# Queries and keys split in place instead of through DRAM, and a second chunk of feed-forward work tied to attention items

## The chip, the cores and the metric

One core of a Trainium2 chip runs the whole program. The metric is device time in microseconds of one execution; the kernel before took 875.44 us (median of 3 runs, 873.63 to 877.91). Engines are named as in the profile: PE (matmuls) with PEld (its weight loads), DVE, ACT, POOL, and SP, which here only issues DMAs. Each engine takes its instructions strictly in the order in which the program lists them, so one that waits holds up all behind it on that engine.

## The reference

Four batches of 576 tokens, 8 heads of 64. Causal attention with a bias from a running sum of gates, then a two-matmul feed-forward mix with a gate, then a mixer over tokens and channels:

```python
scores = scale * np.matmul(q, k.transpose(0, 1, 3, 2))
scores = np.where(causal, -1e9, scores + np.minimum(bias, 0.0))
attn = softmax(scores)
x = np.matmul(attn, v)                       # to [batch, 576, 512]
k = np.maximum((mu_k * x + (1 - mu_k) * x_prev) @ w_k, 0.0)
v = k * k @ w_v
r = sigmoid((mu_r * x + (1 - mu_r) * x_prev) @ w_r)
x = r * v                                    # then the token and channel mixer
```

## The kernel before

**Numbers in two parts.** To get float32 results from PE's faster format (F32R), a number is split in a high part (a copy rounded to F32R) and a low part (the number less its high part). A product is then three matmuls: high by high, high by low, low by high (`products`, L103 to L109). Queries and keys of batches 1 to 3 are split in the same way, but there the three products share two matmuls, since a head has only 64 rows of the 128 that a matmul sums over. X1 holds the high queries and keys in one half of the partitions and in the other half 4 rows for the bias (from ext_d in DRAM) and zeros. X2 holds high queries and low queries against low keys and high keys. `scores` (L294 to L312) issues one matmul on X1 (L307) and one on X2 (L308) for each block. There are two X1 and two X2, used in turn: even visits have the first, odd visits the second.

**Visits and items.** A visit is one head of batches 1 to 3, 24 in all. An item is one block of 128 query rows of a visit. An even visit has five items, of 128, 256, 384, 512 and 576 columns; the fifth holds the last 64 rows of two heads at once, its own and the next visit's, so the odd visit has four. The fifth item's scores come in two parts of 288 columns, and `maskp` masks the second. Each item runs through a chain: scores on PE, `softmax_max` on DVE (L278), the exponential on ACT (L289), the sum's reciprocal (POOL L290, DVE L291), the normalisation on POOL (L292), transposes on PE (L435, L450), their split on ACT and DVE, and the product with the values on PE (L493). Batch 0's attention (L392, L401, L421) comes before and runs unsplit.

**Where queries and keys come from.** Two heads are treated together, in four quarters: queries or keys, 288 columns at a time, 128 partitions. `load` (L227 to L231) brings a quarter from qk to half of a buffer PB. `split` (L233 to L240) makes the high part on ACT (the helper's L75) and the low part on POOL (L239), and SP stores both to hl_d in DRAM (L240). `place` (L260 to L269) later fills a visit's X1 and X2 by four DMAs: the bias rows (L266) and three from hl_d (L267 to L269). PB shares one place (tag HX) with the early heads' queries and keys and with the first chunk's mixed input, so the first load comes after the last matmul on HX.

**Feed-forward work.** Each batch has two chunks of rows (256 and 320). A chunk is 8 `up`, 4 `gate` and 8 half `down` units, 12 matmuls each; its matmuls are at L108, on XK, XR and KK. `mix` (DVE, ACT) makes the input of a chunk from attention's result, so a batch's units can begin when its attention is done. They are spread over the items of the next batch's attention by `todo`, and are what PE does while an item's softmax runs on the other engines. starts and ends (L792) shift the batches' ranges in items.

**What sets the order.** Instructions are written with a place: `with at(x)` gives all inside a priority, and a scheduler, which simulates the engines, lists for each engine what is ready by that priority. An item n has place N0 + n, its transposes N0 + n + 1.5, a feed-forward unit of item n N0 + n + 3. Something of low priority is taken earlier where an engine would stand idle in that simulation. The lists are then fixed, and on the chip each engine follows its own.

Of the kernel before, what the change touches and what calls it, by code (L numbers as in the profile page):

```python
# [8 lines left out]
F32 = mybir.dt.float32  # L9
# [5 lines left out]
ALU = mybir.AluOpType  # L15
# [4 lines left out]
def f32(ap):  # L20
    return ap.bitcast(F32)
# [3 lines left out]
def attention_moe_mixer(  # L25
# [72 lines left out]
    ext_d = dram.tile([G, 4, 2, S], F32, name="ext_d")  # L98
    hl_d = dram.tile([G - H, D, 4, S], F32, name="hl_d")
    y_d = dram.tile([B, DM, S], F32, name="y_d")  # L100
# [21 lines left out]
    VS = v_p.tile([128, NS, 2 * D], F32, name="VS")  # L122
    maskp = v_p.tile([128, S // 2], BF16, name="maskp")

# [16 lines left out]

    X1, X2, PT, VV = {}, {}, {}, {}

    xt = {}

    def constants():
        nc.gpsimd.affine_select(
            out=maskc[:, 512:640], in_=maskc[:, 512:640], pattern=[[-1, 128]],
            compare_op=ALU.is_ge, fill=-8.0e9, base=0, channel_multiplier=1,
        )  # L150
        make_identity(nc, ident)
        nc.gpsimd.memset(maskp, 0.0)
        nc.gpsimd.tensor_copy(maskp[0:TAIL, S // 2 - TAIL:], maskc[0:TAIL, 512:512 + TAIL])
        nc.scalar.dma_start(out=maskp[TAIL:2 * TAIL, S // 2 - TAIL:], in_=maskc[0:TAIL, 512:512 + TAIL])

# [59 lines left out]

    qk_raw = {}

    def stage():
        if "PB" not in act:
            act["PB"] = qk_p.tile([128, 8 * QC], F32, tag="HX", name="PB")  # L220
        return act["PB"]

    def part(y):
        x, c = divmod(y, 2)
        return x, S * c // 2, S * (c + 1) // 2

    def load(i, y):  # L227
        g = visits[i][0]
        x, c0, c1 = part(y)
        t = qk_raw[i, y] = stage()[:, y % 2 * S // 2:(y % 2 + 1) * S // 2]  # L230
        nc.sync.dma_start(out=t, in_=qk[g:g + 2, :, x, c0:c1].rearrange("h d s -> (h d) s"))  # L231

    def split(i, y):  # L233
        g = visits[i][0] - H
        x, c0, c1 = part(y)
        t = qk_raw.pop((i, y))
        e = stage()[:, S + y % 2 * S:S + y % 2 * S + S].rearrange("p (t s) -> p t s", t=2)
        copy("A", e[:, 1].bitcast(F32R), t)
        nc.gpsimd.tensor_tensor(out=e[:, 0], in0=t, in1=e[:, 1], op=ALU.subtract)  # L239
        nc.sync.dma_start(out=hl_d[g:g + 2, :, 2 * x:2 * x + 2, c0:c1].rearrange("h d t s -> (h d) t s"), in_=e)  # L240

# [18 lines left out]
    def place(i):  # L260
        g = visits[i][0]
        t = hl_d[g - H]
        if i < 2:
            X2[i] = x_tile(2 + i, F32R)
        x1, x2 = xs(i)
        nc.sync.dma_start(out=f32(x1[0:4]), in_=ext_d[g])  # L266
        nc.sync.dma_start(out=f32(x1[64:128]), in_=t[:, 1:4:2])  # L267
        nc.sync.dma_start(out=f32(x2[0:64]), in_=t[:, 0:4:3])
        nc.sync.dma_start(out=f32(x2[64:128]), in_=t[:, 1:3])  # L269

# [23 lines left out]
    def scores(i, j):  # L294
        pair = j == NS - 1
        w = 128 * j + (TAIL if pair else 128)
        m = 128
        q0 = 128 * j
        P = p_p.tile([128, w], F32, tag=f"P{j}", name=f"P{j}")
        mx = st_p.tile([128, 2], F32, tag="mx", name="mx")  # L300
        parts = [(0, w // 2), (w // 2, w)] if pair else [(0, w)]
        for x, (c0, c1) in enumerate(parts):
            ps = ps_s.tile([128, 512], F32, tag="s", name="s")
            for e in (1, 0) if pair else (0,):
                x1, x2 = xs(i + e)
                n, a = (TAIL * (1 + e), S - TAIL * (1 + e)) if pair else (128, q0)
                nc.tensor.matmul(ps[0:n, 0:c1 - c0], x1[:, 0, a:a + n], x1[:, 1, c0:c1], start=True, stop=False)  # L307
                nc.tensor.matmul(ps[0:n, 0:c1 - c0], x2[:, 0, a:a + n], x2[:, 1, c0:c1], start=False, stop=True)  # L308
            softmax_max(j, ps, P, mx, x, c0, c1, None if not pair else maskp if x else maskc[:, 0:c1])
        softmax(j, P, mx, x, pair)  # L310
        pst[i, j] = P

# [69 lines left out]
    def late(h, j):  # L382
# [7 lines left out]
        for y, (c0, c1) in enumerate(parts):  # L390
            ps = ps_s.tile([128, 512], F32, tag="s", name="s")
            nc.tensor.matmul(ps[0:m, 0:c1 - c0], x[0:D + 4, 0, q0:q0 + m], x[0:D + 4, 1, c0:c1], start=True, stop=True)  # L392
            softmax_max(j, ps, P, mx, y, c0, c1)
        softmax(j, P, mx, y)
        if j == QC // 128:
# [249 lines left out]
    def attention_item(n):  # L645
        if n < N1:
# [4 lines left out]
            if j == 2 and h > 1 and h % 2 == 0 and h // 2 + 1 < H // 2:  # L651
                with at(N0 + n):
                    late_values(h // 2 + 1)
            if h >= H - 4:
                x = 3 * (h - H + 4) + j - 2
                with at(N0 + n + 0.1):
                    if x >= 4 and x < 8:
                        split(0, x - 4)
                    if x in (2, 3, 4, 5):
                        load(0, x - 2)  # L660
                    if x == 8:
                        load_v(0)
                    if x in (10, 11):
                        load(2, x - 10)
            if h == H - 1 and j == 3:
                with at(N0 + n + 0.2):
                    split_v(0)
            if h == H - 2 and j == 2:
                with at(N0 + n):
                    for x in range(2):  # L670
                        X1[x] = x_tile(x, F32R)
                        nc.gpsimd.memset(f32(X1[x][0:64]), 0.0)
            if h == H - 1 and j == 2:
# [10 lines left out]
        if j == 0 and i + 1 < len(visits):  # L684
            with at(N0 + n):
                place(i + 1)
        if i % 2 == 0:
            with at(N0 + n + 0.1):
                if j < 4 and i + 2 < len(visits):
                    split(i + 2, j)  # L690
                    if j < 2:
                        load(i + 2, 2 + j)
                if j == NS - 1 and i + 2 < len(visits):
                    load_v(i + 2)
        else:
            with at(N0 + n + 0.1):
                if 2 <= j < 4 and i + 3 < len(visits):
                    load(i + 3, j - 2)
            if j == 1 and i + 1 < len(visits):
                with at(N0 + n + 0.2):  # L700
                    split_v(i + 1)
        with at(N0 + n):
# [88 lines left out]
    base = (NS - 2) * H  # L791
    starts, ends = [0, 2, 4, 4], [2, 4, 4, 4]  # L792
    for b in range(B):
# [230 lines left out]
```

## Time and profile before

| | |
|---|---|
| time of the profiled execution | 872.6 us |
| its span, first to last instruction | 870.8 us |
| median of 3 runs | 875.44 us |
| busy share of the span: PE, PEld | 97%, 91% |
| DVE, ACT, POOL | 56%, 52%, 39% |
| mean granted clock of PE | 0.992 |
| DMA traffic | 108.36 MB, mean 124 GB/s |

The page's slices show PE busy nearly throughout, with DVE, ACT and POOL at some 60 to 80% until about 440 us, where attention ends, and falling off afterwards, while the mixer's matmuls fill PE to the end. In a view of waits, a row says which engine, tile and line waited, for what, how many us in total, how often, and the longest. In a view of time, a row has start, duration, engine, line, and in brackets the idle time just before and what ended it. Matmuls are pipelined, so a busy PE is not a PE at its peak.

### The profile page before, as it was taken

The numbers are of one execution on the slowest core, as the hardware profiler recorded it, in microseconds if no ns is written. First come the engines' busy times: TensorE is split into PE (matmuls) and PEld (weight loads), VectorE is DVE, ScalarE is ACT, GpSimd is POOL, SyncE is SP. The second block draws the span as 40 slices with busy tenths as digits, with TensorE's granted clock in tenths as the row PEclk, the third lists the DMA queues.
The fourth block names the chain that finished last, engine by engine and source line by source line (L and its number), as shares of the span: only waits on it lengthen the run. The fifth ranks groups of instructions, "written<-read, shape, count | busy, mean of one in ns | idle before, by whom it ended". The sixth has DMA issues, their size and how long they took to land. (4 is left out here: it accounts for less than half of the span.)

```text
span 870.8 us, 17455 instructions
## 1 busy us (share of the span) xinstructions
PE 840.6 (97%) x6127; PEld 790.5 (91%) x6127; DVE 485.1 (56%) x1352; ACT 452.6 (52%) x1257; POOL 343.4 (39%) x601
## 2 busy tenths in 40 slices
PE   8889998999899999999999999999999999999998
PEld 5656777988789999999999989999999999999998
DVE  5797776565879566985469757951331222222221
ACT  4688766865886656868377865840310221211210
POOL 4565666864785544645256854720000000000000
PEclk9899999999999999999999999999999999999999
DMA  7943778687974244431234746553021112112100
GB/s 191 266 134 88 199 218 230 192 240 210 252 204 133 70 111 117 100 93 41 83 94 129 230 143 217 177 181 94 7 92 54 44 31 74 42 32 73 38 25 26
DMA packets 88024, 108.36 MB, mean 124 GB/s; under 512 B 11152, under 2 KB 71568, under 8 KB 87936
## 3 DMA queue, kind: packets, MB, share of 16 engines
q1 hardware_dynamic: 81408, 91.56, 37.7%
q0 software_dynamic: 4576, 15.08, 5.5%
q8 instruction: 49, 0.80, 0.4%
q10 hardware_dynamic: 1952, 0.60, 0.3%
q14 instruction: 39, 0.32, 0.1%
HBM read 77.74 MB, written 28.90 MB: 122 GB/s over the span
## 5 line engine op out<-in xcount | busy, mean ns | idle before, releaser
L863 ACT ACTIVATE HID<-c 128x256 fp32r<-128x256 f32 (+1 forms) x96 | 39.3, 410 | 220.9 <-PE c L108 220.8
L108 PE MATMUL vd<-KK,WV 128*128 128x256 f32 (+1 forms) x768 | 120.9, 300 | 0.1
L108 PEld LDWEIGHTS vd<-KK,WV 128*128 128x128 f32 x768 | 106.6, 188 | 2.4 <-issue 0.9
L292 POOL TENSOR_SCALAR P<-P,sum 128x128 f32<-128x128 f32 (+4 forms) x148 | 93.6, 636 | 36.2 <-DVE sum L291 30.2
L108 PE MATMUL h<-XK,WK 128*128 128x320 f32 (+1 forms) x672 | 105.9, 303 | 0.7 <-DVE XK L517 0.5
L108 PE MATMUL c<-HID,WV 128*128 128x256 f32 (+1 forms) x768 | 104.9, 291 | 0.0
L108 PE MATMUL c<-U,WK 128*128 128x256 f32 (+1 forms) x768 | 103.2, 291 | 1.4 <-DVE HID L864 1.4
L289 ACT ACTIVATE P<-P,mx 128x128 f32<-128x128 f32 (+4 forms) x148 | 86.9, 588 | 30.3 <-DVE mx L278 23.0
L108 PEld LDWEIGHTS c<-HID,WV 128*128 128x128 f32 x768 | 100.6, 188 | 0.0
L108 PEld LDWEIGHTS c<-U,WK 128*128 128x128 f32 x768 | 98.6, 188 | 1.7 <-DVE HID L864 1.7
L108 PEld LDWEIGHTS h<-XK,WK 128*128 128x128 f32 x672 | 93.8, 189 | 2.1 <-DVE XK L517 0.7
L864 DVE SCALAR_TENSOR_TENSOR HID<-c,HID 128x256 fp32r<-128x256 f32 (+1 forms) x96 | 43.8, 456 | 81.1 <-ACT HID L863 81.0
L278 DVE CUSTOM_DVE_ANT_0 P<-s,maskc 128x128 f32<-128x128 f32 (+4 forms) x148 | 69.1, 478 | 22.1 <-PE t L435 8.4
L928 DVE TENSOR_TENSOR ut<-c,ut 128x256 f32<-128x256 f32 (+1 forms) x32 | 14.6, 458 | 119.3 <-PE c L108 112.0
L529 POOL TENSOR_TENSOR KK<-k,KK 128x256 fp32r<-128x256 f32 (+1 forms) x64 | 55.8, 877 | 19.8 <-ACT k L528 18.7
L108 PE MATMUL r<-XR,WR 128*128 128x320 f32 (+1 forms) x384 | 60.0, 299 | 0.0
L290 POOL TENSOR_SCALAR sum<-sum 128x1 f32<-128x1 f32 (+1 forms) x148 | 32.4, 219 | 67.6 <-ACT P L289 57.2
L108 PE MATMUL c<-HID,WR 128*128 128x256 f32 (+1 forms) x384 | 54.8, 291 | 0.0
L108 PEld LDWEIGHTS r<-XR,WR 128*128 128x128 f32 x384 | 52.8, 188 | 1.1 <-ACT raw L614 0.4
L108 PE MATMUL c<-U,C1A 128*128 128x256 f32 (+1 forms) x384 | 52.8, 296 | 0.1
L108 PEld LDWEIGHTS c<-U,C1A 128*128 128x128 f32 x384 | 51.5, 190 | 0.3 <-ACT U L913 0.3
L108 PEld LDWEIGHTS c<-HID,WR 128*128 128x128 f32 x384 | 51.3, 188 | 0.0
(133 smaller groups left out, 1658.4 us busy)
## 6 DMA issues: line engine op xcount, KB each, us to landing
X<-hl_d SPq DMA_DIRECT2D x72, 288.0 KB
hl_d<-PB SPq DMA_DIRECT2D x48, 288.0 KB
raw<-in_moe_w_ch_dram POOLq DMA_DIRECT2D x48, 256.0 KB, 3.3
PB<-in_qk_dram SPq DMA_DIRECT2D x48, 144.0 KB
yt<-y_d SPq DMA_DIRECT2D x16, 288.0 KB
u_d<-yt SPq DMA_DIRECT2D x16, 288.0 KB
raw<-in_moe_w_k_dram SPq DMA_DIRECT2D x8, 512.0 KB
raw<-in_moe_w_v_dram SPq DMA_DIRECT2D x16, 256.0 KB
```

The source lines that it names most:

```text
L108: nc.tensor.matmul(ps, a, b, start=first and i == 0, stop=last and i == n - 1)
L278: nc.vector.tensor_tensor_reduce(out=P[0:m, c0:c1], in0=ps[0:m, 0:c1 - c0], in1=mask[0:m], scale=-scale, scalar=3.0e38 if x == 0 else mx[0 ...
L289: nc.scalar.activation(out=P[0:m, 0:w], in_=P[0:m, 0:w], func=AF.Exp, bias=mx[0:m, x:x + 1], scale=-1.0, accum_out=sm[0:m, 0:1])
L290: nc.gpsimd.tensor_scalar(out=sm[0:m, 0:1], in0=sm[0:m, 0:1], scalar1=1e-9, scalar2=1.0, op0=ALU.add, op1=ALU.mult)
L292: nc.gpsimd.tensor_scalar(out=P[0:m, 0:w], in0=P[0:m, 0:w], scalar1=sm[0:m, 1:2], scalar2=1.0, op0=ALU.mult, op1=ALU.mult)
L529: nc.gpsimd.tensor_tensor(out=kk[:, 1, m, 0:n], in0=t[:, 0:n], in1=f32(kk[:, 0, m, 0:n]), op=ALU.subtract)
L863: nc.scalar.activation(out=hi, in_=ps, func=AF.Relu)
L864: nc.vector.scalar_tensor_tensor(out=lo, in0=ps, scalar=0.0, in1=f32(hi), op0=ALU.max, op1=ALU.subtract)
L928: nc.vector.tensor_tensor(out=t, in0=ps, in1=t, op=ALU.add)
```

## The change

`split`, hl_d and the quarters go. `load` brings a head's whole queries and keys in one DMA to one half of the partitions of a buffer RQ. `place` splits from there: ACT copies the high part straight into X1, a DMA copies it on to its place in X2, and POOL writes the low part into X2 in two pieces of 288 columns; keys first, then queries. Then it issues the load for the visit after the next one. Even visits have their queries and keys in the lower half of X1, odd ones in the upper half. The fifth item's two parts become 512 and 64 columns. Batch 0's second chunk is spread over 43 items instead of 37, batch 1's units begin 6 items later, and the PE instructions of batch 0's second chunk may not come ahead of the last score matmul of their item (`issue_after`).

```diff
-    maskp = v_p.tile([128, S // 2], BF16, name="maskp")
+    maskp = v_p.tile([128, TAIL], BF16, name="maskp")
+    heads = []
...
-    def load(i, y):
-        g = visits[i][0]
-        x, c0, c1 = part(y)
-        t = qk_raw[i, y] = stage()[:, y % 2 * S // 2:(y % 2 + 1) * S // 2]
-        nc.sync.dma_start(out=t, in_=qk[g:g + 2, :, x, c0:c1].rearrange("h d s -> (h d) s"))
-
-    def split(i, y):
-        g = visits[i][0] - H
-        x, c0, c1 = part(y)
-        t = qk_raw.pop((i, y))
-        e = stage()[:, S + y % 2 * S:S + y % 2 * S + S].rearrange("p (t s) -> p t s", t=2)
-        copy("A", e[:, 1].bitcast(F32R), t)
-        nc.gpsimd.tensor_tensor(out=e[:, 0], in0=t, in1=e[:, 1], op=ALU.subtract)
-        nc.sync.dma_start(out=hl_d[g:g + 2, :, 2 * x:2 * x + 2, c0:c1].rearrange("h d t s -> (h d) t s"), in_=e)
+    def sides(i):
+        a, z = slice(0, D), slice(D, 2 * D)
+        return (a, z) if i % 2 == 0 else (z, a)
+
+    def raw_qk():
+        if "RQ" not in act:
+            act["RQ"] = qk_p.tile([128, 8 * QC], F32, tag="HX", name="RQ")
+        return act["RQ"][:, 0:2 * S].rearrange("p (t s) -> p t s", t=2)
+
+    def load(i):
+        nc.sync.dma_start(out=raw_qk()[sides(i)[0]], in_=qk[visits[i][0]])
...
     def place(i):
         g = visits[i][0]
-        t = hl_d[g - H]
...
-        nc.sync.dma_start(out=f32(x1[0:4]), in_=ext_d[g])
-        nc.sync.dma_start(out=f32(x1[64:128]), in_=t[:, 1:4:2])
-        nc.sync.dma_start(out=f32(x2[0:64]), in_=t[:, 0:4:3])
-        nc.sync.dma_start(out=f32(x2[64:128]), in_=t[:, 1:3])
+        a, z = sides(i)
+        rq = raw_qk()[a]
+        nc.sync.dma_start(out=f32(x1[z][0:4]), in_=ext_d[g])
+        for y in (1, 0):
+            nc.scalar.activation(out=x1[a, y], in_=rq[:, y], func=AF.Copy)
+            high, low = (z, a) if y else (a, z)
+            nc.sync.dma_start(out=f32(x2[high, y]), in_=f32(x1[a, y]))
+            for c in range(2):
+                cs = slice(S * c // 2, S * (c + 1) // 2)
+                nc.gpsimd.tensor_tensor(out=x2[low, y, cs], in0=rq[:, y, cs], in1=f32(x1[a, y, cs]), op=ALU.subtract)
+        if i + 2 < len(visits):
+            load(i + 2)
...
-        parts = [(0, w // 2), (w // 2, w)] if pair else [(0, w)]
+        parts = [(0, 128 * j), (128 * j, w)] if pair else [(0, w)]
...
-                nc.tensor.matmul(ps[0:n, 0:c1 - c0], x2[:, 0, a:a + n], x2[:, 1, c0:c1], start=False, stop=True)
+                mm = nc.tensor.matmul(ps[0:n, 0:c1 - c0], x2[:, 0, a:a + n], x2[:, 1, c0:c1], start=False, stop=True)
...
+        heads.append(mm.ins)
...
-            if h >= H - 4:
-                x = 3 * (h - H + 4) + j - 2
+            if h == H - 3 and j == 2:
                 with at(N0 + n + 0.1):
...
+                    load(0)
+                    load(1)
+            if h == H - 2 and j == 4:
+                with at(N0 + n + 0.1):
+                    load_v(0)
...
-                        nc.gpsimd.memset(f32(X1[x][0:64]), 0.0)
+                        nc.gpsimd.memset(f32(X1[x][sides(x)[1]]), 0.0)
...
-        if i % 2 == 0:
+        if i % 2 == 0 and j == NS - 1 and i + 2 < len(visits):
             with at(N0 + n + 0.1):
-                if j < 4 and i + 2 < len(visits):
-                    split(i + 2, j)
-                    if j < 2:
-                        load(i + 2, 2 + j)
-                if j == NS - 1 and i + 2 < len(visits):
-                    load_v(i + 2)
...
-    starts, ends = [0, 2, 4, 4], [2, 4, 4, 4]
+    starts, ends = [0, 8, 4, 4], [8, 4, 4, 4]
+    tied = set()
...
+                tied.add(id(acts))
...
-            with at(N0 + n + 3):
+            with at(N0 + n + 3), tc.issue_after(heads[n - 0]) if id(acts) in tied else ExitStack():
                 run(acts)
```

## Rows read from the trace of the kernel before

**Rows 1.** Busy us (and instructions) of each engine by stretch; clock, DMA share, GB/s
```profile
core 0: us, PE busy (x) PEld busy (x) DVE busy (x) ACT busy (x) POOL busy (x), PEclk, DMA share, GB/s
125.00:275.00 150.00, 138.70 (x978) 127.36 (x978) 105.77 (x343) 108.01 (x307) 103.77 (x190) 0.99 0.77 211
...
275.00:425.00 150.00, 149.93 (x1135) 148.19 (x1135) 104.03 (x330) 103.50 (x280) 74.16 (x143) 1.00 0.34 85
...
437.00:600.00 163.00, 158.20 (x1125) 155.73 (x1124) 112.75 (x244) 102.78 (x295) 88.71 (x125) 1.00 0.52 162
```

**Rows 2.** Waits of ACT, POOL and PE from 125 to 275 us
```profile
ACT PB L75 <- DMA PB<-in_qk_dram: 27.5, 20, 3.6
...
POOL PB L239 <- ACT PB L75: 16.5, 12, 3.2
...
PE s L308 <- DMA X<-hl_d: 4.1, 3, 2.3
```

**Rows 3.** Waits of SP's queue from 87 to 275 us
```profile
SPq L240 <- POOL PB L239: 31.4, 16, 4.7
```

**Rows 4.** In order of time, 224 to 246 us: one late load
```profile
225.40 0.34 SPq L231 DMA_DIRECT2D PB<-in_qk_dram  x1
...
227.62 0.44 ACT L75 ACTIVATE PB<-PB 128x288 fp32r<-128x288 f32 x1 [0.99 <-DMA PB<-in_qk_dram]
...
228.20 0.79 POOL L239 TENSOR_TENSOR PB<-PB 128x288 f32<-128x288 f32 x1 [1.29 <-ACT PB L75]
...
229.40 0.33 PE L435 MATMUL t<-ident,P 128*128 128x128 f32 x1 [1.34 <-POOL P L292]
```

**Rows 5.** In order of time, 143.5 to 147.5 us: one direct wait for X
```profile
145.57 0.60 SPq L269 DMA_DIRECT2D X<-hl_d  x1
...
147.04 0.19 PEld L308 LDWEIGHTS s<-X 128*128 128x128 f32 x1 [2.42 <-issue]
```

**Rows 6.** Busy time by 25 us, columns as in rows 1
```profile
125.00:150.00 25.00, 22.58 (x143) 18.24 (x143) 16.81 (x56) 14.57 (x42) 16.57 (x32) 0.96 0.81 217
150.00:175.00 25.00, 25.00 (x176) 24.56 (x175) 15.02 (x48) 22.28 (x64) 20.60 (x36) 0.97 0.70 194
...
225.00:250.00 25.00, 22.12 (x161) 19.87 (x159) 20.90 (x73) 21.69 (x65) 18.10 (x35) 1.00 0.85 234
```

**Rows 7.** Groups by line and shape: ACT's and POOL's prices
```profile
L239 POOL TENSOR_TENSOR PB<-PB 128x288 f32<-128x288 f32 x48 | 40.0, 835 | 23.9 <-ACT PB L75 18.6 <-DMA y_d<-e 3.7 <-DVE sum L291 0.6
...
L75 ACT ACTIVATE PB<-PB 128x288 fp32r<-128x288 f32 x48 | 21.2, 441 | 30.7 <-DMA PB<-in_qk_dram 29.8 <-POOL PB L239 0.3 <-issue 0.2
...
L289 ACT ACTIVATE P<-P,mx 64x576 f32<-64x576 f32 x8 | 6.3, 787 | 0.9 <-DVE sum L291 0.9
L75 ACT ACTIVATE WK<-raw 128x512 fp32r<-128x512 f32 x8 | 5.4, 677 | 1.3 <-DVE raw L616 1.3
```

**Rows 8.** Waits of SP's queue from 275 to 440 us
```profile
SPq L266 <- PE s L308: 30.6, 7, 10.5
```

**Rows 9.** In order of time, 224 to 246 us: X between two even visits
```profile
226.91 0.29 PE L308 MATMUL s<-X 128*64 128x288 f32 x1
...
227.11 0.27 SPq L266 DMA_DIRECT2D X<-ext_d  x1
...
233.54 0.31 PE L307 MATMUL s<-X 128*128 128x128 f32 x1
```

**Rows 10.** Groups by line and shape: DVE's prices of the masked maximum
```profile
L278 DVE CUSTOM_DVE_ANT_0 P<-s,maskc 128x512 f32<-128x512 f32 x32 | 21.9, 683 | 2.9 <-PE t L435 1.8 <-PE t L401 0.4 <-PE s L392 0.3
...
L278 DVE CUSTOM_DVE_ANT_0 P<-s,maskc 128x128 f32<-128x128 f32 x32 | 9.1, 283 | 11.1 <-PE t L435 6.6 <-PE idle L162 2.4 <-PE s L338 1.7
...
L278 DVE CUSTOM_DVE_ANT_0 P<-s,maskp,mx 128x288 f32<-128x288 f32 x12 | 6.1, 510 | 3.1 <-PE s L308 3.1
```

**Rows 11.** Busy time by 12.5 us of L108's matmuls and weight loads alone
```profile
200.00:212.50 12.50, 7.95 (x46) 6.94 (x46) 1.00 0.66 201
...
225.00:237.50 12.50, 1.22 (x6) 0.83 (x6) 1.00 0.99 263
```

More of the change, by code (lines that the diff above doesn't have):

```diff
@@ L98, in attention_moe_mixer @@
     ext_d = dram.tile([G, 4, 2, S], F32, name="ext_d")
-    hl_d = dram.tile([G - H, D, 4, S], F32, name="hl_d")
     y_d = dram.tile([B, DM, S], F32, name="y_d")
@@ L152, in constants @@
         nc.gpsimd.memset(maskp, 0.0)
-        nc.gpsimd.tensor_copy(maskp[0:TAIL, S // 2 - TAIL:], maskc[0:TAIL, 512:512 + TAIL])
-        nc.scalar.dma_start(out=maskp[TAIL:2 * TAIL, S // 2 - TAIL:], in_=maskc[0:TAIL, 512:512 + TAIL])
+        nc.gpsimd.tensor_copy(maskp[0:TAIL], maskc[0:TAIL, 512:512 + TAIL])
+        nc.scalar.dma_start(out=maskp[TAIL:2 * TAIL], in_=maskc[0:TAIL, 512:512 + TAIL])
     def behind(p, cell):
@@ L214, in xs @@
         return X1[i % 2], X2[i % 2]
[L216 to L225, printed above, removed]
-    def load(i, y):
-        g = visits[i][0]
-        x, c0, c1 = part(y)
-        t = qk_raw[i, y] = stage()[:, y % 2 * S // 2:(y % 2 + 1) * S // 2]
-        nc.sync.dma_start(out=t, in_=qk[g:g + 2, :, x, c0:c1].rearrange("h d s -> (h d) s"))
-    def split(i, y):
-        g = visits[i][0] - H
-        x, c0, c1 = part(y)
-        t = qk_raw.pop((i, y))
-        e = stage()[:, S + y % 2 * S:S + y % 2 * S + S].rearrange("p (t s) -> p t s", t=2)
-        copy("A", e[:, 1].bitcast(F32R), t)
-        nc.gpsimd.tensor_tensor(out=e[:, 0], in0=t, in1=e[:, 1], op=ALU.subtract)
-        nc.sync.dma_start(out=hl_d[g:g + 2, :, 2 * x:2 * x + 2, c0:c1].rearrange("h d t s -> (h d) t s"), in_=e)
+    def sides(i):
[7 more added lines that the diff above has]
+        nc.sync.dma_start(out=raw_qk()[sides(i)[0]], in_=qk[visits[i][0]])
     def load_v(i):
@@ L391, in late @@
             ps = ps_s.tile([128, 512], F32, tag="s", name="s")
-            nc.tensor.matmul(ps[0:m, 0:c1 - c0], x[0:D + 4, 0, q0:q0 + m], x[0:D + 4, 1, c0:c1], start=True, stop=True)
+            mm = nc.tensor.matmul(ps[0:m, 0:c1 - c0], x[0:D + 4, 0, q0:q0 + m], x[0:D + 4, 1, c0:c1], start=True, stop=True)
             softmax_max(j, ps, P, mx, y, c0, c1)
+        heads.append(mm.ins)
         softmax(j, P, mx, y)
@@ L653, in attention_item @@
                     late_values(h // 2 + 1)
-            if h >= H - 4:
-                x = 3 * (h - H + 4) + j - 2
+            if h == H - 3 and j == 2:
                 with at(N0 + n + 0.1):
[L657 to L664, printed above, removed]
+                    load(0)
[3 more added lines that the diff above has]
+                    load_v(0)
             if h == H - 1 and j == 3:
@@ L686, in attention_item @@
                 place(i + 1)
-        if i % 2 == 0:
+        if i % 2 == 0 and j == NS - 1 and i + 2 < len(visits):
             with at(N0 + n + 0.1):
-                if j < 4 and i + 2 < len(visits):
-                    split(i + 2, j)
-                    if j < 2:
-                        load(i + 2, 2 + j)
-                if j == NS - 1 and i + 2 < len(visits):
-                    load_v(i + 2)
[L695 to L701, printed above, removed]
+                load_v(i + 2)
+        if i % 2 and j == 1 and i + 1 < len(visits):
+            with at(N0 + n + 0.2):
+                split_v(i + 1)
         with at(N0 + n):
```

## The prediction

> **What bounds the kernel now.** I read the 40 slices of the page first, then busy time by stretch, then who waited for whom, then one wait in order of time. The reader is to see two neighbouring stretches of 150 us that do nearly the same work: pieces of attention with feed-forward matmuls between them. In the later one (275 to 425 us) TensorE idles 150 - 149.9 = 0.1 us and its weight loads idle 150 - 148.2 = 1.8 us. In the earlier one (125 to 275 us) they idle 11.3 and 22.6 us [rows 1]. After attention (437 to 600 us) TensorE is busy 158.2 of 163 us and waits for weights that the change does not touch [rows 1]. So the prize lies in the earlier stretch, and the later one is what can be spoilt.
>
> What sets the two apart is the splitting of queries and keys. It runs in the first stretch and is over by the second, because its results are parked in DRAM and nothing holds it back. There ACT sat 27.5 us waiting for raw queries and keys to land, POOL sat 16.5 us behind ACT for the same pieces [rows 2], and SP sat 31.4 us (from 87 us on) in front of the stores to hl_d until POOL had subtracted [rows 3]. It feeds itself: SP stands before a store, the next load stands behind that store, ACT stands before the late load, and softmax stands behind ACT. One such case in order of time: a load is issued at 225.40, ACT starts on it at 227.62 after 0.99 us idle, POOL subtracts from 228.20 to 228.99 after 1.29 us idle, only then comes the normalisation that PE's transpose needs, and PE starts at 229.40 after 1.34 us idle [rows 4]. PE waits directly for the transfers into X three times, 4.1 us in all [rows 2]; the longest runs from the transfer's issue at 145.57 to the weight load at 147.04 [rows 5]. The granted clock was 0.96 from 125 to 150 us and 0.97 from 150 to 175 us, so a part of both ran at the lower of the two levels, 1.2 GHz [rows 6].
>
> **The change part by part.**
>
> *Loads and the round trip through DRAM.* By the code, a visit moved 288 KB in, 576 KB out to hl_d and 864 KB back into X; now 288 KB in and 2 x 144 KB from X1 to X2, so 1728 KB become 576 KB. SP's issues per visit fall from 2 loads, 2 stores and 4 transfers into X to 1 load, 1 bias transfer and 2 copies. The new load is issued when POOL has read the previous raw half, a whole visit before it is needed; a load of half that size took 2.2 us from issue to ACT's start in the case above (225.40 to 227.62 [rows 4]), so ACT's 27.5 us of waiting for loads and POOL's 16.5 us behind it have no cause left. What becomes late next is place itself (below). SP still waits for POOL before a load; behind it stand stores to y_d, values and the next bias transfer, none of them due within that visit. The first load still waits for the buffer of tag HX, as before: no change there.
>
> *The split itself.* POOL: 48 subtractions of 128x288 at 835 ns (40.1 us) become 96 of 64x288. A POOL row costs by its free size, not its partitions (ACT's and POOL's 64-row forms are no cheaper, as ACT's 64x576 at 787 ns shows), so 96 x 835 = 80.2 us, 40.1 us more. ACT: 48 copies of 128x288 at 441 ns (21.2 us) become 48 of 64x576, between 677 ns (128x512, the same kind of copy) and 787 ns (64x576, an exponential) [rows 7]; I take 730, nearer to the copy: 35.0 us, 13.8 us more. And they are spread differently. X has two buffers, so a visit can be split only when its X is free: about 24 visits in 275 us, or 13 in 150 us. The earlier stretch then holds 13 x 4 x 0.835 = 43.4 us of POOL instead of 31.7 (38 x 0.835), little changed at 103.8 - 31.7 + 43.4 = 115.5 of 150; the later one goes from 74.2 to 117.6 us on POOL and from 103.5 to 103.5 + 13 x 2 x 0.73 = 122.5 on ACT [rows 1]. Today this work is hidden behind PE there, and at 78% and 82% it mostly still is; if that cover goes, the later stretch looks like the earlier one of today and idles 11.3 us. If PE stays ahead, it costs nothing. Between 0 and 11.3 I take 4, because PE idles 0.1 us there now and has feed-forward matmuls to run. A gain there is excluded: there is no idle time to win.
>
> *The wait that is added.* Before, X being free was waited for by SP (30.6 us on L266 from 275 to 440 us [rows 8]), which held nobody. Now ACT's copy into X1 waits for it, and POOL's subtraction waits for ACT; behind them stand exponentials, copies of transposed pieces and normalisations. Room, from one even visit: the last score on the old X starts at 226.91, SP sends the first transfer at 227.11, the next even visit's first score starts at 233.54 [rows 9], so 6.6 us. The chain is one ACT copy and four subtractions, 0.73 + 4 x 0.835 = 4.1 us, the second copy and both DMAs beside them, plus what stands ahead on POOL. It fits with 2.5 us to spare; its price is in the 4 us above.
>
> *The pair's last piece.* Two parts of 288 columns become 512 and 64. DVE: at most 2 x 510 = 1020 ns now; 683 and at most 283 (the 128x128 form bounds the 64-column one), at most 966, after [rows 10], 12 times. PE streams the same columns. Nothing, either way.
>
> *Batch 0's second chunk.* It is 240 matmuls by the code (96 up, 48 gate, 96 down). While they last, 12.5 us hold 46 feed-forward matmuls, as from 200 us; from 225 us, with them used up and batch 1 hardly begun, they hold 6 [rows 11]. The tie forbids taking them early, and the last fifth moves behind batch 1's attention. This moves PE work without changing its sum: what the slice from 225 us gains in cover, the slices before it lose. Bounds: it could give back or cost the 2.9 us that PE idles where cover is thinnest (25 - 22.12 between 225 and 250 us [rows 6]); I take 0.
>
> **Sum.** Visible idle time of the earlier stretch 11.3 us, of which 4.1 is the direct wait for X: -11.3. Later stretch: +4. Net -7.3. The profiled execution took 872.6 us (span 870.8), 2.8 us under the median of 875.4: 872.6 - 7.3 = 865.3, against the median **868.1 us**.
>
> Rows first: PE's idle time in the earlier stretch is 11.3 us and PE's weight loads' 22.6 us [rows 1]. The Trainium skill (Perfetto Trace Analysis, section Identifying the Most-Contended Engine) says that matmul busy time flatters because matmuls are pipelined, and that the weight loads' busy share is the measure. By the first the prize is 11.3 us, by the second 22.6; I sum by the first and keep the second as a rival.
>
> **The rivals.**
>
> *The whole shortfall comes back.* If the time that PE's weight loads idle is the true loss, the earlier stretch becomes like the later: 22.6 - 1.8 = 20.8 us. 872.6 - 20.8 + 4 = 855.8, against the median 858.6. For it: in the later stretch nearly all of it is absent. Against it: some of it in the earlier one belongs to batch 0's own matmuls and to POOL's load, which stays. Chance 0.12.
>
> *No change.* Only the direct waits for X go (4.1 us) and POOL's load takes it back (4): 872.5, against the median 875.3. For it: between 150 and 175 us PE was busy all 25 us although the splits ran [rows 6]. It would also be so if the tie did not bind and the new loads came late; against that, the loads have a visit's time and the second chunk does run out early today [rows 11]. Chance 0.22.
>
> *Slower: place turns into the wait.* Place: ACT's copy into X1, at the head of ACT's queue before PE has done its last score on that X. Then ACT and POOL inherit what SP waits today, up to 30.6 us in the later stretch, which is as much as ACT's 27.5 in the earlier one. Price: the earlier stretch keeps its idle time but for 4.1 us, the later gets 11.3: 872.6 - 4.1 + 11.3 = 879.8, against the median 882.6. It decides when queueing on ACT and POOL takes the 4.1 us chain beyond 6.6 us. The Trainium skill (SBUF — State Buffer, section SBUF: two separate sides) says that GpSimd and VectorE instructions with two SBUF inputs lock each other out of a shared port; by that rule 40 us more of POOL would also slow VectorE, and no row here tells how much. Chance 0.16.
>
> **How the numbers follow.** Forecast 0.50, with a range of its own of 862 to 874 (the 4 us at its ends, 0 and 11.3, rounded, with part of the tie's 2.9 us). A measurement of this kernel tells about 0.5% from no change, 4.4 us, so faster means under 871.1 and slower over 879.8. Faster: 0.45 of the forecast's 0.50 and 0.12, 0.57. Same: 0.05 and 0.20 of the no-change case, 0.25. Slower: 0.02 and 0.16, 0.18. The range 855 to 880 takes in the forecast, no change and most of the full gain; it leaves out the slower case.
>
> **What would show it.** Right: ACT's waits for raw queries and keys gone, PE's idle time from 125 to 275 us under 4 us, POOL near 78% busy and PE still over 97% from 275 to 425 us, attention's last score some 7 us earlier. Wrong: ACT waiting at the copy into X1 for PE, PE waiting at the scores for X, or POOL's normalisation as what PE's transposes wait for in the later stretch. If PE's matmuls before 225 us thin out and its idle time there grows, the tie costs what I set at 0.

## The result and the profile after

The kernel after takes 879.85 us (median of 8 runs, 877.71 to 883.16), the one before in the same job 875.49: ratio 1.0053 [1.0033, 1.0073]. It is slower where a gain was forecast; 879.85 lies at the upper end of the range. The profiled execution after took 883.16 us (span 881.4), 10.6 us of span over the one before. It is the slowest of its eight, and the one before (872.6 us) was under all of its eight, so the profiles lie further apart than the medians (4.4 us).

Waits first, since they were the reason for the forecast. From 87 to 275 us (us in total, times, longest): the first three rows are waits that went up, POOL's first and PE's are all that is left of the kinds in [rows 2], POOL's second is new; then SP's queue:

```profile
DVE P L271 <- PE t L430: 11.3, 8, 4.1
DVE PT L449 <- ACT PT L448: 10.2, 4, 7.4
...
ACT XK L511 <- DVE t L510: 9.4, 5, 5.1
...
POOL X L260 <- ACT X L255: 4.4, 3, 2.0
...
POOL X L260 <- PE s L386: 2.3, 1, 2.3
...
PE s L301 <- DMA X<-X: 0.4, 1, 0.4
```

```profile
SPq L253 <- PE s L301: 51.3, 10, 16.4
SPq L226 <- POOL sum L283: 15.0, 8, 3.2
```

ACT's 27.5 us behind loads have no row any more, POOL's 16.5 us behind ACT are 4.4, PE's 4.1 us for transfers into X are 0.4. POOL's 2.3 us behind PE is the added wait for X to be free, late in batch 0's attention. SP waits longer than in [rows 3], but it holds up little: only PE's 0.4 us are a wait for a copy within X. What went up are DVE's waits in attention, for PE's transposes (3.0 us in the kernel before, 125 to 275 us) and for ACT's copies of transposed pieces, and ACT's wait for DVE's `mix` (1.7 us before, 87 to 275 us). Next, groups by line and shape (busy us, mean ns), against [rows 7, 10]:

```profile
L260 POOL TENSOR_TENSOR X<-RQ,X 64x288 fp32r<-64x288 f32 x96 | 78.8, 839 | 13.1 <-ACT X L255 8.0 <-PE s L386 2.3
...
L255 ACT ACTIVATE X<-RQ 64x576 fp32r<-64x576 f32 x48 | 30.1, 675 | 2.2 <-PE s L300 1.6
L271 DVE CUSTOM_DVE_ANT_0 P<-s,maskc 128x512 f32<-128x512 f32 x44 | 29.5, 684 | 13.3 <-PE t L430 8.1 <-PE t L396 3.0 <-ACT P L282 1.0
...
L271 DVE CUSTOM_DVE_ANT_0 P<-s,maskp,mx 128x64 f32<-128x64 f32 x12 | 3.3, 277 | 0.7 <-PE s L301 0.5
```

Each price is near its forecast: 839 ns for POOL (835), 675 for ACT (730), 684 and 277 for DVE. So neither the waits that were to go nor these durations were wrong, and the time must be lost elsewhere. Busy time by stretch, columns as in [rows 1]:

```profile
125.00:275.00 150.00, 140.02 (x957) 126.49 (x956) 105.26 (x332) 106.63 (x281) 113.91 (x199) 0.97 0.30 76
275.00:425.00 150.00, 147.60 (x1105) 142.93 (x1104) 110.12 (x335) 114.86 (x308) 106.87 (x186) 1.00 0.23 61
437.00:600.00 163.00, 157.05 (x1122) 153.64 (x1122) 114.08 (x247) 105.09 (x300) 90.54 (x129) 1.00 0.54 169
...
150.00:175.00 25.00, 23.02 (x133) 21.05 (x134) 11.27 (x42) 18.39 (x48) 16.30 (x30) 0.86 0.20 48
```

In the earlier stretch PE's idle time fell only from 11.3 to 10.0 us and the granted clock from 0.99 to 0.97; it was 0.86 from 150 to 175 us (0.97 before [rows 6]). In the later one PE idles 2.4 us in place of 0.1, its weight loads 7.1 in place of 1.8. Over both, PE's busy time falls by 1.0 us (288.63 to 287.62), its weight loads' by 6.1 (275.55 to 269.42). The Trainium skill (Perfetto Trace Analysis, section Identifying the Most-Contended Engine) calls matmul busy time no good measure of a kernel's headroom and names the weight loads' busy share as one to use instead; here the trace agrees, because 1.0 us is too little for what follows. The last score on X starts at 423.6 us, against 415.6 in the kernel before (first row before, then after):

```profile
L308 PE MATMUL s<-X x144: 222/296/522, 128.8 to 415.6; 128*128 128x128 f32 x24, 128*128 128x256 f32 x24, 128*128 128x384 f32 x24, 128*128 128x512 f32 x24
...
L301 PE MATMUL s<-X x144: 192/317/525, 134.3 to 423.6; 128*128 128x512 f32 x36, 128*128 128x128 f32 x24, 128*128 128x256 f32 x24, 128*128 128x384 f32 x24
```

So 8.0 of the 10.6 us are lost before attention ends, where the forecast had 7 us won. But 5.5 of the 8.0 are there already at the first score on X (134.3 for 128.8), although batch 0's last score starts only 1.0 us later (126.7 for 125.7). PE is busy in between, and POOL is in the next visit's four subtractions, with the sum of batch 0's last head behind them:

```profile
127.87 3.59 POOL L260 TENSOR_TENSOR X<-RQ,X 64x288 fp32r<-64x288 f32 x4
...
131.58 0.19 POOL L283 TENSOR_SCALAR sum<-sum 128x1 f32<-128x1 f32 x1
```

Busy time on either side of 175 us, first before, then after:

```profile
125.00:175.00 50.00, 47.58 (x317) 42.80 (x317) 31.83 (x103) 36.86 (x104) 37.17 (x67) 0.97 0.76 206
175.00:275.00 100.00, 91.13 (x663) 84.56 (x662) 73.94 (x241) 71.15 (x204) 66.60 (x124) 1.00 0.77 214
```

```profile
125.00:175.00 50.00, 45.52 (x277) 38.07 (x276) 27.39 (x91) 32.91 (x85) 35.34 (x61) 0.93 0.28 67
175.00:275.00 100.00, 94.51 (x682) 88.42 (x681) 77.87 (x242) 73.73 (x197) 78.57 (x139) 0.98 0.32 81
```

From 175 us on the kernel after is ahead, by 3.9 us of weight loads; in the 50 us before it has lost 4.7. The late start stands in the traces of e4 and e13 too (first matmul on X at 133.9 and 133.1 us); no run isolated its cause.

### The profile page after: what moved, and what is told of

Its sections match the earlier page's. It is cut to its first block, busy times and chain, and to the rows that moved or that the text cites. A ratio compares the mean times of both kernels' runs of the same rounds, so it can differ in the third digit from the quotient of the medians.

```text
span 881.4 us, 17425 instructions
## 1 busy us (share of the span) xinstructions
PE 850.3 (96%) x6127; PEld 793.7 (90%) x6127; DVE 491.0 (56%) x1352; ACT 464.1 (53%) x1257; POOL 382.1 (43%) x649
## 5 line engine op out<-in xcount | busy, mean ns | idle before, releaser
L271 DVE CUSTOM_DVE_ANT_0 P<-s,maskc 128x128 f32<-128x128 f32 (+4 forms) x148 | 72.0, 498 | 36.9 <-PE t L430 18.2
L260 POOL TENSOR_TENSOR X<-RQ,X 64x288 fp32r<-64x288 f32 x96 | 78.8, 839 | 13.1 <-ACT X L255 8.0
```

The costliest lines, as they stand in the source:

```text
L260: nc.gpsimd.tensor_tensor(out=x2[low, y, cs], in0=rq[:, y, cs], in1=f32(x1[a, y, cs]), op=ALU.subtract)
L271: nc.vector.tensor_tensor_reduce(out=P[0:m, c0:c1], in0=ps[0:m, 0:c1 - c0], in1=mask[0:m], scale=-scale, scalar=3.0e38 if x == 0 else mx[0 ...
```

## The experiments

Every kernel was timed against the kernel before in the same job, which had medians of 874.93 to 875.68 us. Line numbers in the rows are each kernel's own, so the same line of code can stand some lines lower or higher.

| run | kernel | us | ratio, interval |
|---|---|---|---|
| e1 | split alone | 887.32 | 1.0128 [1.0093, 1.0164] |
| e2 | split and parts | 884.09 | 1.0088 [1.0057, 1.0120] |
| e3 | before + tie and shift | 879.33 | 1.0043 [1.0022, 1.0064] |
| e4 | split, tie and shift, old parts | 874.72 | 0.9992 [0.9971, 1.0013] |
| e5 | e4, low parts on DVE | 895.70 | 1.0237 [1.0208, 1.0266] |
| e6 | e4, each subtraction on POOL twice | 929.19 | 1.0618 [1.0594, 1.0643] |
| e7 | e4 without the shift | 892.99 | 1.0201 [1.0177, 1.0225] |
| e8 | after, queries first | 880.99 | 1.0059 [1.0038, 1.0079] |
| e9 | e4 without the tie | 881.03 | 1.0055 [1.0030, 1.0079] |
| e10 | before + shift | 878.48 | 1.0025 [1.0009, 1.0041] |
| e11 | e4, two long subtractions for four | 881.12 | 1.0061 [1.0039, 1.0084] |
| e12 | before + parts | 880.99 | 1.0052 [1.0033, 1.0072] |
| e13 | e4, keys' low parts left out | 865.81 | 0.9895 [0.9873, 0.9916] |
| e14 | before, each subtraction twice | 885.21 | 1.0124 [1.0101, 1.0148] |
| e15 | before, no addition of 1e-9 | 878.72 | 1.0037 [1.0018, 1.0056] |
| e16 | e4, no addition of 1e-9 | 872.58 | 0.9972 [0.9956, 0.9988] |
| e17 | e4, split given to two items | 875.03 | 1.0000 [0.9984, 1.0016] |
| e18 | e17, no addition of 1e-9 | 873.43 | 0.9982 [0.9965, 1.0000] |

"Shift" is the new `starts` and `ends`, "tie" is `issue_after`, "parts" are 512 and 64 columns in place of 288 and 288.

### The three parts of the change, one by one

e1 is the kernel after with these lines as before (and maskp with them); e2 leaves the new parts in, e4 leaves the new starts, ends and tie in.

```diff
-        parts = [(0, 128 * j), (128 * j, w)] if pair else [(0, w)]
+        parts = [(0, w // 2), (w // 2, w)] if pair else [(0, w)]
-    starts, ends = [0, 8, 4, 4], [8, 4, 4, 4]
+    starts, ends = [0, 2, 4, 4], [2, 4, 4, 4]
-            with at(N0 + n + 3), tc.issue_after(heads[n - 0]) if id(acts) in tied else ExitStack():
+            with at(N0 + n + 3):
```

> The direct split alone: loads, place and RQ as after; the tie, the shifted ranges and the pair's parts as before. Theory 1 (the split, moved into the later stretch of attention and bound to X coming free, costs what the removed waits give): about as slow as the whole change, 3 to 7 us over before, PE's weight loads idle 5 us or more from 275 to 425 us. Theory 2 (the split gains as forecast and the tie with the shifted ranges eats it): 5 to 9 us under before. Theory 3 (each part costs about nothing and the list of instructions just fell differently): within 2 us of before.

> The direct split and the pair's parts of 512 and 64 columns, without the tie and the shifted ranges. Theories 1 and 2 both expect the time of the direct split alone, within 2 us, since the parts were priced at nothing; if the parts cost, it is over that by more than 2 us, and the scores' rows show it.

> The kernel before with the tie and the shifted ranges alone. Theory 1: within 2 us of before, since PE's work only moves. Theory 2: 9 us or more over before, with PE's idle time before 225 us grown.

> The whole change with the pair's parts left at 288 and 288 columns. Theory 1 and theory 2: the whole change's time, 4 us over before, within 2 us. If the parts of 512 and 64 columns cost, it is 2 us or more under the whole change.

Measured: the split alone costs 11.6 us (887.32 less the job's 875.68), more than any of its three theories had; with tie and shift it costs nothing (874.72). So tie and shift are worth 12.6 us to the split, while on the kernel before they cost 3.7. The parts cost 5.1 us on e4 (879.85 for 874.72), but gave 3.2 back on the split alone (e2). The next two separate tie and shift on e4, e10 has the shift alone on the kernel before.

```diff
-    starts, ends = [0, 8, 4, 4], [8, 4, 4, 4]
+    starts, ends = [0, 2, 4, 4], [2, 4, 4, 4]
```

> Split and tie with the ranges of items as before (the second chunk over 37 items, batch 1 from 2 items after attention's end instead of 8), parts of 288. If the tie is what turned the split alone (11.6 us over before) into split and tie (1 us under): within 3 us of split and tie. If it is the shift: near the split alone, 8 us or more over before. In between if both.

> Split and tie, parts of 288, without the tie: the ranges of items shifted by 6, nothing bound to an item. Theory S (the shift, which puts batch 1's units behind the end of attention of batch 0's follower instead of in front of it on PE's list, is what takes the split from 887 to 875, and the tie is a loss, 893 against 887): at or under split and tie, 868 to 875. Theory T (only tie and shift together help: the shift because the tie leaves work that has to go somewhere): near the split alone, 882 or more.

> The kernel before with the shifted ranges alone. Theory S: 3 us or more under before (tie and shift on it cost 3.7 us, and the tie costs 5.7 on the split alone). Theory T: within 2 us of before or slower.

On the split alone (887.32) the shift gives back 6.3 us (881.03 without the tie), between its two theories; the tie costs 5.7 (892.99 without the shift); both together give 12.6. On the kernel before the shift costs 3.0 (878.48 for 875.50). The traces show a part of why. Busy time of PE and PEld in feed-forward matmuls alone by 12.5 us (then granted clock, DMA share, GB/s), as in [rows 11]; first e1:

```profile
212.50:225.00 12.50, 1.23 (x6) 0.84 (x6) 1.00 0.43 102
225.00:237.50 12.50, 0.29 (x2) 0.30 (x2) 1.00 0.35 82
237.50:250.00 12.50, 9.55 (x53) 8.86 (x52) 0.73 0.29 67
```

The same of e9 (no tie):

```profile
225.00:237.50 12.50, 0.00 (x0) 0.00 (x0) 1.00 0.32 78
237.50:250.00 12.50, 9.16 (x45) 8.23 (x45) 0.73 0.28 72
```

The same of e7 (no shift):

```profile
225.00:237.50 12.50, 1.48 (x6) 1.04 (x6) 0.95 0.33 76
237.50:250.00 12.50, 6.88 (x49) 6.33 (x50) 0.91 0.18 50
```

And of e4 (both):

```profile
212.50:225.00 12.50, 5.39 (x35) 5.02 (x36) 1.00 0.33 87
225.00:237.50 12.50, 7.84 (x54) 7.06 (x54) 1.00 0.47 116
237.50:250.00 12.50, 7.28 (x54) 6.52 (x53) 1.00 0.11 26
```

Without the tie PE has next to no feed-forward matmuls for 25 us (8 in e1), and when they return the granted clock is 0.73: a mean of the levels 2.4 and 1.2 GHz, so (1 - 0.73) / 0.5 = 54% of 12.5 us at the lower. With the tie but no shift (e7) the thin stretch is 12.5 us and the clock 0.95 in it and 0.91 after it. With both, 35, 54 and 54 matmuls lie there and the clock stays 1.00. That a thin stretch lowers the clock is not shown: the kernel before has 6 such matmuls from 225 to 237.5 us [rows 11] and 1.00 in the next 12.5 us:

```profile
237.50:250.00 12.50, 6.48 (x48) 6.00 (x48) 1.00 0.70 205
```

Nor is this stretch the whole loss. From 125 to 275 us PE runs 997 matmuls in e4, 961 in e1, 934 in e9 and 930 in e7. After the last score on X, e1 and e7, which lack the shift, need another 461.5 and 465.3 us, e4 457.4 and e9 456.3. So e9 loses its time before 275 us, e1 and e7 a part of theirs behind attention, and what costs them there was not looked into.

### POOL's added work

e5 moves the subtractions to DVE, e6 does each a second time into a spare tile, e11 makes two of 576 columns out of four of 288:

```diff
-                nc.gpsimd.tensor_tensor(out=x2[low, y, cs], in0=rq[:, y, cs], in1=f32(x1[a, y, cs]), op=ALU.subtract)
+                nc.vector.tensor_tensor(out=x2[low, y, cs], in0=rq[:, y, cs], in1=f32(x1[a, y, cs]), op=ALU.subtract)
```

> Split and tie, parts of 288 as in the run before, but the four subtractions of a visit on DVE instead of POOL. Theory P (the 3.4 us that place takes on POOL stand in front of normalisations, and that is what the later stretch loses): 4 to 8 us under split and tie, about 868, with the stretch from the 288th to the 576th down matmul back at 154 us from 157. Theory L (time follows the order in which the lists fall, not POOL's load): within 3 us of split and tie, either way. Theory D (DVE, busy 106 of 150 us there, is as tight as POOL): 3 us or more slower than split and tie.

> Split and tie, parts of 288, with each of POOL's subtractions done a second time into a spare tile: 40 instructions' worth of 838 ns in each 10 visits more, 80 us in all. Theory P: the first 40 us cost about 5 us in the later stretch, so 80 more cost 10 us or more, 885 or above. Theory L: within 4 us of split and tie, since POOL still has room (107 + 43 of 150 us leaves none in the later stretch, so even here some loss is possible).

> Split and tie, parts of 288, with POOL's four subtractions of 288 columns done as two of 576: estimated 1.43 us each from POOL's 128x256 (774 ns) and 128x512 (1299 ns) forms, so some 12 us less POOL in all, in blocks that are 0.6 us longer. Theory P (POOL's load, steep: 80 us more cost 54): 3 to 8 us under split and tie. If the length of a block counts more than the sum: slower than split and tie.

Twice as many subtractions cost 54.5 us (929.19 less 874.72) for 80 us of POOL; DVE does one in 507 ns and still the kernel is 21.0 us slower; two long ones take 1447 ns each, 9 us less POOL in all, and the kernel is 6.4 us slower. So the work is not free, but its busy time is not its price. One visit of e4 in order of time (start, us, engine, line):

```profile
167.43 3.19 POOL L260 TENSOR_TENSOR X<-RQ,X 64x288 fp32r<-64x288 f32 x4
...
169.32 0.72 ACT L282 ACTIVATE P<-P,mx 128x512 f32<-128x512 f32 x1
...
170.69 0.87 POOL L524 TENSOR_TENSOR KK<-k,KK 128x320 fp32r<-128x320 f32 x1
...
171.66 0.19 POOL L283 TENSOR_SCALAR sum<-sum 128x1 f32<-128x1 f32 x1
...
172.10 0.15 DVE L284 RECIPROCAL sum<-sum 128x1 f32<-128x1 f32 x1
...
174.04 0.72 POOL L285 TENSOR_SCALAR P<-P,sum 128x512 f32<-128x512 f32 x1
```

The exponential ends at 169.32 + 0.72 = 170.04. POOL is in its four subtractions until 167.43 + 3.19 = 170.62, then takes a feed-forward piece, and comes to the sum at 171.66 and to the normalisation at 174.04, behind values' low parts: 4 us with no wait of POOL recorded, because POOL is busy nearly all the time. That is how a gain can go without a wait that names it. In this one case only the first 0.6 us are the subtractions themselves; the rest is other work that came to POOL in the meantime.

e13 takes the added load away by leaving out keys' low parts (the product of high queries and low keys is then missing from the scores), and e14 puts the same load on the kernel before:

```diff
+        if i < 2:
+            nc.gpsimd.memset(f32(x2[a, 1]), 0.0)
...
-                nc.gpsimd.tensor_tensor(out=x2[low, y, cs], in0=rq[:, y, cs], in1=f32(x1[a, y, cs]), op=ALU.subtract)
+                if y == 0:
+                    nc.gpsimd.tensor_tensor(out=x2[low, y, cs], in0=rq[:, y, cs], in1=f32(x1[a, y, cs]), op=ALU.subtract)
```

```diff
         nc.gpsimd.tensor_tensor(out=e[:, 0], in0=t, in1=e[:, 1], op=ALU.subtract)
+        nc.gpsimd.tensor_tensor(out=scr, in0=t, in1=e[:, 1], op=ALU.subtract)
```

> Split and tie without the change of parts (874.7 us as measured), and the low parts of the keys are left out: their place in X2 holds zeros, so the product of high queries and low keys is missing from the scores. POOL then has 48 subtractions in place of 96, 40 us less, as much as in the kernel before; the place block on POOL is 1.7 us long in place of 3.4. Theory P (POOL's added blocks eat the gain): by half of the price of doubling them (54.5 us for 80 us) at most 27 us less, at least the 7.3 us of the forecast: 855 to 868. Theory O (the gain is lost by the new order of the work and the later start of attention, whatever POOL does): 872 to 877.

> The kernel before, with each of its 48 low-part subtractions on POOL done a second time into a spare tile: 40 us more POOL in the earlier stretch, where the splits run, and nothing else. Theory P: POOL's added work stands between an item's reciprocal and its normalisation and is paid for in part: 880 to 895. Theory O: POOL was at 69% there and stays under 85%, so the work is hidden: 874 to 878.

Both fall in the ranges of the theory that named POOL's load as the cause. 40 us less POOL on the split are worth 8.9 us (865.81 for 874.72), 40 us more on the kernel before cost 9.9 (885.21 for 875.29). Busy time by stretch, first e4, then e13, then e14:

```profile
125.00:275.00 150.00, 142.28 (x997) 129.83 (x996) 109.28 (x345) 110.37 (x293) 115.99 (x204) 0.98 0.31 77
275.00:425.00 150.00, 149.35 (x1129) 147.24 (x1128) 106.14 (x329) 114.35 (x301) 107.62 (x183) 1.00 0.24 61
```

```profile
125.00:275.00 150.00, 145.97 (x1058) 137.31 (x1059) 113.69 (x371) 117.47 (x312) 101.98 (x193) 0.98 0.34 82
275.00:425.00 150.00, 148.51 (x1114) 146.34 (x1113) 102.54 (x309) 108.21 (x290) 83.86 (x150) 1.00 0.23 59
```

```profile
125.00:275.00 150.00, 136.00 (x896) 121.31 (x895) 98.37 (x317) 103.40 (x293) 127.94 (x216) 0.94 0.78 209
275.00:425.00 150.00, 148.55 (x1140) 146.74 (x1139) 111.11 (x344) 105.45 (x289) 81.98 (x156) 1.00 0.37 93
```

The price falls in the earlier stretch: with POOL at 102 us of 150 PE's weight loads are busy 137.3 us, at 116 us 129.8; in the later stretch they differ by 0.9. From 125 to 175 us they are busy 42.6 us in e13, as in the kernel before (42.8), and 40.1 in e4. Since e13's attention begins about as late as e4's, the late start alone does not cost those 50 us. e13's last score starts at 407.9 us, 7.7 before the kernel before's.

### The order of the work, and a version below both

e12 has the parts alone, e8 turns round which half of a visit is split first; neither adds an instruction.

```diff
-        parts = [(0, w // 2), (w // 2, w)] if pair else [(0, w)]
+        parts = [(0, 128 * j), (128 * j, w)] if pair else [(0, w)]
```

```diff
-        for y in (1, 0):
+        for y in (0, 1):
```

> The whole change with queries split ahead of keys in place, the same instructions in another order. Theory L (5 us either way is how the lists fall): 3 us or more away from the whole change's 879.9, either way. Theory B (the pair's parts of 512 and 64 cost the 5 us between split and tie and the whole change, by a longer chain from PE to DVE, 0.33 us for each of 12 pairs): within 2 us of the whole change.

> The kernel before with the pair's parts of 512 and 64 columns alone. Theory B (the chain through one pair's two parts is longer: PE 0.92 us, then DVE 0.68 and 0.28, against PE and DVE overlapped by halves, some 0.3 us for each of 12 pairs, and it is on the path): 2 to 5 us over before. Theory L (the parts cost nothing, and 5 us between split and tie and the whole change are how the lists fall): within 2 us of before.

e8 is 1.1 us from the kernel after, so its time does not hang on that one order. The parts alone cost 5.5 us, a little over the 2 to 5 of the theory that names a longer chain. In e12 DVE sat idle before its maxima for PE's transposes 18.7 us, 14 times, against 8.4 us, 9 times, in the kernel before (first its row, then e12's):

```profile
DVE P L278 <- PE t L435: 8.4, 9, 2.0
```

```profile
L278 DVE CUSTOM_DVE_ANT_0 P<-s,maskp,mx x12: 271/278/285, 142.2 to 412.8; 128x64 f32<-128x64 f32 x12
...
  PE t L435: 18.7, 14
```

That maxima stand later in the lists, behind other items' transposes, and that the last piece of 64 columns is what the planner reacts to, is argued, not shown. Since the sign turned round in e2, the size is not a property of the parts alone.

e15 and e16 leave out POOL's addition of 1e-9 to the sums, in the kernel before and in e4; e17 and e18 give keys' split to the first item of a visit and queries' to the second:

```diff
-        nc.gpsimd.tensor_scalar(out=sm[0:m, 0:1], in0=sm[0:m, 0:1], scalar1=1e-9, scalar2=1.0, op0=ALU.add, op1=ALU.mult)
```

```diff
-        if j == 0 and i + 1 < len(visits):
+        if j < 2 and i + 1 < len(visits):
             with at(N0 + n):
-                place(i + 1)
+                place(i + 1, (1 - j,))
```

> The kernel before without POOL's addition of 1e-9 to each sum of exponentials (a sum is at least about 1, so the float32 sum stays the same): 148 instructions of 0.22 us, 32 us less POOL, and one change of engines less in each item's chain (ACT, DVE, POOL in place of ACT, POOL, DVE, POOL). Theory P: POOL is the middle of the chain in the earlier stretch, so 5 to 11 us less: 864 to 870. Theory O: an item's chain has slack against the list of the work: 873 to 877.

> Split and tie without the change of parts (874.7 us as measured), and without POOL's addition of 1e-9. Theory P: the split is held back by POOL's load, so it gains more from this than the kernel before does, 8 to 16 us: 859 to 867, the fastest of all so far. Theory O: no more than the kernel before gains from it, 0 to 3 us: 872 to 875.

> Split and tie without the change of parts (874.7 us as measured), with the split of a visit given to two items: keys with the first item of the visit before, queries with its second. The same instructions; a block on POOL is two subtractions, 1.7 us, in place of four, 3.4 us. Theory block (a normalisation waits behind four subtractions): the block was half of what leaving out the keys' low parts gave back (8.9 us), so 866 to 871. Theory sum (POOL's total counts, wherever it stands): 872 to 877.

> The same with POOL's addition of 1e-9 to the sums left out (872.6 us as measured with the split in one item). Theory block: 864 to 869, below both kernels. Theory sum: 870 to 875.

32 us less POOL made the kernel before 3.4 us slower and e4 2.1 faster: both expectations had it wrong for the kernel before, and e4's gain is far under what its load predicted, though within the other theory's 0 to 3 us. So POOL's total load does not by itself set the time, and taking out the 0.22 us pieces does not free the items. e16, at 872.58 us [0.9956, 0.9988], is the fastest that leaves out no product, below both kernels by little; e18 (873.43) cannot be told from it. e17 did not bring its condition about: in the rows of POOL 16 groups of four subtractions in a row are left (17 in e4), since the planner put the halves together again, as here:

```profile
260.96 1.36 POOL L286 TENSOR_SCALAR P<-P,sum 128x576 f32<-128x576 f32 x2
262.41 3.78 POOL L261 TENSOR_TENSOR X<-RQ,X 64x288 fp32r<-64x288 f32 x4
266.26 0.73 POOL L525 TENSOR_TENSOR KK<-k,KK 128x256 fp32r<-128x256 f32 x1
```

Whether shorter blocks would cost less than the same work in one stays open.

## Why the prediction was wrong

*Loads and the round trip through DRAM*: right on the waits. The three went from 27.5, 16.5 and 4.1 us to none, 4.4 and 0.4, and no new load wait came. With tie, shift and POOL's load as before this is worth 9.5 us (e13, 865.81 for 875.29), near the 11.3 that were taken.

*The split itself*: the durations were right (839 and 675 ns); the step that failed is "little changed at 103.8 - 31.7 + 43.4 = 115.5 of 150". POOL's busy time there came out as worked out (113.9, in e4 116.0), but it was given no price, since the busy share was low. The price is 8.9 us, and it falls there, not in the later stretch, where 4 were set: PE idles 0.65 us there in e4. The mistake is to price POOL by its share and not by what stands behind the added work; that these are the normalisations is shown in one case only.

*The wait that is added*: right between visits. ACT's copy into X1 waited 1.6 us for PE's scores, and 2.5 us of room were enough. The room was worked out between two even visits; the first visits, where X comes free only as batch 0's last heads end, were left out; there POOL waits 2.3 us and the first score on X comes 5.5 us later, though no run shows how much of this is the wait. The rival on the slower side came out in its sign but not in its mechanism: ACT's copy hardly waits, POOL's subtractions are in the way.

*The pair's last piece*: "Nothing, either way" failed. It costs 5.1 us on top of e4 and 5.5 alone. The durations were right, so busy time bounds nothing here; how the cost comes about is open (below).

*Batch 0's second chunk*: "This moves PE work without changing its sum" failed by its size, 12.6 us on the split against bounds of 2.9 either way. [rows 11] held the evidence: cover that ran out from 225 us. What was left out is that with the split the stretch without cover is longer (25 us in e1) and that the clock after it can be low, 0.73 in e1 and e9. The sign that was named for a cost of the tie came by half: from 150 to 225 us PE runs 465 matmuls in place of 486, but idles 4.0 us in place of 5.0.

**Sum.** -9.5 for the waits with tie and shift, +8.9 for POOL, +5.1 for the parts give +4.5; measured are 879.85 - 875.49 = +4.4. Forecast were -11.3, +4 and 0. The two terms differ by 4.9 and 5.1 us, and the first by 1.8. The terms are the steps of one path from kernel to kernel (before, e13, e4, after), so they add up by construction; what the runs show is the price of each step on the one ahead of it. The terms are not independent (the parts give 3.2 us back on e1): by another path the same end is reached from e1 as +11.6, -12.6 and +5.1, with 0.3 left over from the jobs' medians. And each step also plans the lists anew: four small edits of the kernel before moved it by 3.0 to 5.5 us, so a single price of that size, that of the parts above all, may be no more than this.

*No change* had its exchange right (the waits' gain is taken back by POOL's load): that is e4, at 874.72, though with 9.5 against 8.9 us and not 4.1 against 4. The parts made it slower on top. *The whole shortfall comes back* was wrong in its size, but right in its measure: the loss shows in the weight loads' busy time, not in PE's.

By the rule of the Trainium skill on the shared port (SBUF — State Buffer, section SBUF: two separate sides), GpSimd's work would also lengthen VectorE's instructions with two SBUF inputs. The rows bear that out: the four forms of DVE's subtraction in `mix` take 31.0 us before, 32.6 after and 33.2 in e6, which has 120 us more of POOL's subtractions than the kernel before, and the multiply-add ahead of it goes up more (before, after, e6), while the maxima of 128x512, which take the scores from PSUM, keep their 683 ns (684 after):

```profile
L515 DVE SCALAR_TENSOR_TENSOR t<-xt,omu,t 128x256 f32<-128x256 f32 (+1 forms) x64 | 38.1, 603 | 0.6
...
L510 DVE SCALAR_TENSOR_TENSOR t<-xt,omu,t 128x256 f32<-128x256 f32 (+1 forms) x64 | 41.3, 651 | 0.5
...
L513 DVE SCALAR_TENSOR_TENSOR t<-xt,omu,t 128x256 f32<-128x256 f32 (+1 forms) x64 | 47.4, 745 | 0.6
```

So a part of POOL's price may be paid on DVE. It is hardly the most of it: DVE's three operations of `mix` take 105.6 us in e4 and 102.4 in e13, 3.2 us apart where the time is 8.9 apart, and 111.4 in e16, which is no slower than e4. No run separates the two.

**Left open.** How the added work on POOL becomes 8.9 us, by normalisations behind it or by DVE's longer instructions. Why the first score on X comes late. Why the parts change sign between e1 and e4, and why four small edits of the kernel before (e3, e10, e12, e15) each made it 0.25 to 0.52% slower, e15 with less work. The lists are planned anew each time; no run held a list fixed and changed one duration.

## What to carry to other kernels

A wait that goes is only a gain if the work that replaces it does not stand in the next chain: ask of each added instruction on a half-busy engine what is queued behind it, and price it by that item's delay, not by the engine's share. Where matmuls of one stage cover the latency of another, look for the stretch in which the cover runs out, and read the granted clock in it and after it. Where new work waits for a buffer, look at its first use too, not only at the steady case. And where lists are planned by a simulation, give every edit that changes a duration a range of some 0.5% in either direction, even one that adds no work.

## What was not expected of the hardware

PE's granted clock can be low when the work is back: 1.00 from 212.5 to 237.5 us in e1 with 8 feed-forward matmuls in 25 us, then 0.73 with 53 in 12.5; the kernel before keeps 1.00 after its own thin 12.5 us. A subtraction of 64x288 takes 839 ns on POOL and 507 on DVE, but on DVE the same 96 cost 21.0 us more in time (e5). DVE's multiply-add of two SBUF tiles grew from 603 to 745 ns on average with 120 us more of POOL's subtractions (e6), its maxima of scores in PSUM did not (683 and 687 ns). The price of added POOL work in `place` is steep and grows: 8.9 us for the first 40 us (e13 to e4), 54.5 for 80 us more (e6).
